# Attention loop of a four-layer MQA/Hedgehog kernel: smaller turns where no other work is mixed in, feature spills issued one transfer per tick, and the state update placed before the query normalization

## The chip, the cores and the metric

The kernel runs on one core of a Trainium2 chip. The metric is the device time of one execution in microseconds. A core has a matrix engine (TensorE, PE in the profile, with its weight loads as PEld), a vector engine (VectorE, DVE), a scalar engine (ScalarE, ACT), GpSimd (POOL) and a sync engine (SyncE, SP) whose queue issues the DMAs of this kernel. Each engine works through its own instructions in order and waits on semaphores that the others set.

## The reference

The input is a sequence of 2048 tokens of width 576. Four residual layers follow each other, A, B, A, B, each on a layer-normalized input. A is attention with 32 query heads of width 18 and one shared key and value head (MQA). B is a linear attention with a learned feature map (Hedgehog).

```python
def _A_ref(x, wq, wk, wv, wo):
    q = (x @ wq).reshape(B, S, H, Dh)          # per head
    k = x @ wk; v = x @ wv                     # one head for all
    scores = einsum("bhqd,bkd->bhqk", q, k) * (Dh ** -0.5)
    p = softmax(scores)
    return einsum("bhqk,bkd->bhqd", p, v) @ wo

def _B_ref(x, wqkv, w_phi, wo):
    q, k, v = x @ wqkv                          # per head
    pq = einsum("bhsd,hdf->bhsf", q, w_phi); pk = einsum("bhsd,hdf->bhsf", k, w_phi)
    phi_q = concat([softmax(pq), softmax(-pq)]); phi_k = concat([softmax(pk), softmax(-pk)])
    kv = einsum("bhsf,bhsd->bhfd", phi_k, v); z = einsum("bhsf->bhf", phi_k)
    return (phi_q @ kv) / (phi_q @ z + 1e-6) @ wo
# x = x + A(ln(x)); x = x + B(ln(x)); x = x + A(ln(x)); x = x + B(ln(x))
```

## The kernel before

The work is done in two passes of one A and one B each. In a pass, `attend` runs the attention of A over 4 chunks of 512 queries and 8 groups of 4 heads in each chunk, 32 groups in all. The first group is done ahead of it, so `attend` has 31 groups. A group goes through 16 tiles of 128 keys. A tile is done in two **units** of two heads: a unit is two score matmuls into one `sc` buffer of PSUM (there are three such buffers), and one exponential on ScalarE from `sc` into a tile `pt` in SBUF (L960, 128x1024). When both units of a tile are done, `values` adds their product with the values to the group's accumulator, four matmuls side by side (L738). 31 groups of 32 units are 992 units in a pass.

The main loop of `attend` (L973 to L982) makes one **step** of six units at a time: three units of scores (`BURST`), the value sums of all tiles that were complete before them, two calls of `tick`, three more units, then `fill`, and value sums again unless `fill` issued a lot of work; then a third `tick`. The order of TensorE's instructions is exactly the order in which this loop records them (`in_order`). The order on the other engines comes from a scheduler. So TensorE's row of work in a step without other work is: three units, two tiles of sums, three units, one tile of sums.

`fill` takes work out of the deque `bulk`: projections and the like that are mixed into the attention. For each finished chunk, `after_chunk` puts `chunk_work` into `bulk`. It makes the output projection of A for the chunk (`output`, 8 fills), turns the residual into the tokens of B (`flip_tokens`, `fetch_tokens`, `split_tokens`), and then runs `mix`: for each of the 4 token tiles the keys, the values and the queries of B (2 fills each), the state update (`update_state`, 32 small matmuls on L526 and an addition to `kv` on VectorE), the softmax of the query features (`feature_end`) and the transfer of the features to DRAM (`block_transpose`: a transposition on VectorE and four DMAs, `phi<-pht` in the profile). All this uses one spare PSUM bank at a time. Weights for it are loaded by generators in the deque `loads`, one step of a generator per tick; a weight tile comes by DMA into one of two buffers `wstage` and is split by VectorE into a high and a low part (`wchi` and `wclo` for the query weights `wpq` and the output weights `wo`).

When a group's sums are done, `finish_group` copies the accumulator to `osb` (L870), gets the reciprocal of the denominators by way of DRAM (`rd`, `den_rows`, `parts`), multiplies, and sends the result with four to nine DMAs into `on` (`pack`, `on<-parts`). It goes on by one stage per tick. After the last group of a chunk it waits some more ticks and then puts the chunk's work into `bulk`. The queries of the next group are fetched when a group's first scores are recorded (`qst<-qd`, `qst<-mxd`, eight DMAs); there are two buffers `qst`.

So there are two kinds of steps: mixed ones, while `bulk` holds work, and pure ones, while it is empty. The fourth chunk of a pass is done after the attention in another way that the change does not touch.

Of the kernel before, what the change touches and what calls it, by code (L numbers as in the profile page):

```python
# [60 lines left out]
def kernel(ctx, tc, x_in, wq, wk, wv, wo, wqkv, w_phi, wob, out):  # L61
# [459 lines left out]
    def update_state(e, vb, st, ps):  # L521
        phi = e.rearrange("p h s d -> p (h s d)")
        pk = ps.tile([P, NG * 2 * DH], F32, name="ps")
        for h in range(H):
            g, j = divmod(h, GH)
            T.matmul(pk[32 * j : 32 * j + 32, g * 2 * DH : (g + 1) * 2 * DH],  # L526
                     vb[:, h * (DH + 1) : h * (DH + 1) + 32], phi[:, h * 2 * DH : (h + 1) * 2 * DH],
                     start=True, stop=True)
            if j == GH - 1 and g < NG - 1:
                yield 145  # L530
        with tc.high_priority():
            V.tensor_add(st["kv"], st["kv"], pk)
        yield -145
# [41 lines left out]
    def block_transpose(blocks, src, dst):  # L575
        V.transpose(blocks, src)
        for q in range(P // 32):
            rows = slice(q * 32, (q + 1) * 32)
            nc.sync.dma_start(dst[:, rows].rearrange("(b f) t -> f b t", f=32),
                              blocks[rows, :].rearrange("f (b t) -> f b t", t=32))  # L580

    def flip_tokens(i):
        rstd, bias = ln_stats([i])[i]
        xn = bw.tile([P, H, 2, DH], F32, name="featq").rearrange("p h s d -> p (h s d)")[:, :D]
        V.tensor_scalar(xn, xres[i], rstd, bias, op0=ALU.mult, op1=ALU.add)
        blocks = bw.tile([P, NKG, P], F32, name="pht").rearrange("p a b -> p (a b)")
        block_transpose(blocks[:, :D], xn, flipped[i % TPC])

    def fetch_tokens(i):
        xt = bw.tile([P, KT * P], F32, name="xn").rearrange("p (a b) -> p a b", b=P)  # L590
        src = flipped[i % TPC]
        nc.sync.dma_start(xt[:, 0:4, :], src[:512].rearrange("(k p) t -> p k t", p=P))
        for half in range(2):
            nc.sync.dma_start(xt[half * 64 : half * 64 + 64, 4, :], src[512:])
        return xt
# [5 lines left out]
        V.tensor_sub(xs[64:P, 4, :], xt[64:P, 4, :], xs[64:P, 4, :].bitcast(F32))  # L601
        return xs

    def mix(tiles, fetched, xs, st, ps, spill, loads):
        for n, i in enumerate(tiles):
            ek, eq = (bw.tile([P, H, 2, DH], F32, name=tag) for tag in ("featk", "featq"))
            vb = yield from keys_values(i, xs, ek, st, ps, V)
            while loads:
                yield STAGE
            yield from queries(xs, eq, st, ps, V)  # L610
            if n < len(tiles) - 1:
                xs = split_tokens(fetched)
                if n < len(tiles) - 2:
                    fetched = fetch_tokens(tiles[n + 2])
            for b in range(2):
                feature_end(eq, b, V)
            yield from update_state(ek, vb, st, ps)
            blocks = bw.tile([P, NKG, P], F32, name="pht").rearrange("p a b -> p (a b)")
            block_transpose(blocks[:, : 2 * D], eq.rearrange("p h s d -> p (h s d)"), spill[i])

    def last_mix(n, i, stats, st, sp, ps, spill):
        xn = layer_norm(i, stats, bw if n % 2 else sp, A, "xn" if n % 2 else "xo")
# [222 lines left out]
    def attend(layer, st, a1o, extra, after_chunk, chunks):  # L845
# [11 lines left out]
        with ctx1:  # L857
# [5 lines left out]
                def tile(self, shape, dtype, name):  # L863
                    return bank(*homes[1], shape)
            acc, on = {groups[0]: st["acc0"]}, {}
            urgent, bulk, loads = deque(), deque(), deque()

            def finish_group(c, g):
                osb = a1.tile([P, CW], F32, name="osb", bufs=1)
                V.tensor_copy(osb, acc[c, g])  # L870
# [12 lines left out]
                parts = a1.tile([P, 2, CW], F32R, name="parts", bufs=1)  # L883
                den = parts[:, 1, :].bitcast(F32)
                nc.sync.dma_start(den, rows[:, None, :].to_broadcast([GH, 32, CW]))
                yield STAGE
                yield STAGE
                V.tensor_mul(osb, osb, den)  # L888
                split(parts[:, 0, :], parts[:, 1, :], osb, V, V)
                yield STAGE  # L890
                yield STAGE
                pack(on[c].bitcast(F32), parts.bitcast(F32), g)
                if g == NG - 2:
                    for _ in range(6):
                        yield STAGE
                    bulk.append(after_chunk(c, on[c], Spare(), loads))
                yield STAGE

            def values(c, g, t, pt):
# [13 lines left out]
                urgent.append(f)  # L913

            def tick():
                for queue in (urgent, loads):
                    if queue and next(queue[0], DONE) is DONE:
                        queue.popleft()

# [51 lines left out]
                    in_order()  # L971

            while at[0] < len(units):  # L973
                sums(scores(BURST))
                tick()
                tick()
                ready = scores(BURST)
                spent = fill()
                in_order()
                if spent < HEAVY:  # L980
                    sums(ready)
                tick()  # L982
# [5 lines left out]
            for queue in (bulk, loads):  # L988
                for gen in queue:
                    run(gen)  # L990

# [71 lines left out]
    for layer in range(LAYERS):  # L1063
# [3 lines left out]
        with tc.tile_pool(name="a1o", bufs=2) as a1o:  # L1067
# [27 lines left out]
            def after_chunk(c, on, ps, loads, layer=layer):  # L1095
                return chunk_work(c, on, ps, loads, layer)

            def chunk_work(c, on, ps, loads, layer):
# [12 lines left out]
                loads.append(load_wpq())  # L1111
                yield from mix(tiles, fetched, xs, st, ps, spills[layer], loads)
                loads.append(load_wo())

            attend(layer, st, a1o, extra, after_chunk, chunks)
# [109 lines left out]
```

## Time and profile before

| | us |
|---|---|
| median of 3 runs | 2777.47 (2773.98 to 2779.59) |
| the profiled execution | 2775.14 |
| its span | 2773.3 |
| busy in it: TensorE / ScalarE / VectorE | 2646.9 / 2190.3 / 1243.3 |
| exponentials of the attention (L960) | 1984, 1874.8 busy |
| mean granted TensorE clock | 0.989 |

In a row of the waits stand the engine and line, whom it waited for, the microseconds in total, how often, and the longest. A row of a group ends in busy time and mean duration in nanoseconds, then the idle time before its instructions with what ended it. In a timeline stand the start, the duration of the merged row, engine, line, operation, tiles and count, and in brackets the idle time before. A row of windows has the stretch, its length, and for each engine its busy time with the number of instructions; behind them the granted clock, the DMA share and GB/s.

### The profile page before, as it was taken

Reading aid. Unit: us, or ns where it says so; the run is one execution under the profiler, and the core shown is the slowest. Engines: PE = TensorE matmul, PEld = TensorE weight load, DVE = VectorE, ACT = ScalarE, POOL = GpSimd, SP = SyncE. Lnnn points to the kernel's source line nnn. Section 1 sums busy time; section 2 is a strip of 40 time slices with the busy share of each in tenths; the row PEclk is TensorE's granted clock in tenths of the full one; section 3 lists DMA queues with packets and bytes.
Section 4 is the critical chain, followed back from the end, with each engine's and each line's share of the span. In section 5 each row is a group of like instructions: output and inputs, shape, how many; then the busy total and the mean of one; then the engine's idle time right before and its main releaser. Section 6 shows DMA issues by size and latency. Waiting matters only on the chain. (4 is left out here: it accounts for less than half of the span.)

```text
span 2773.3 us, 55536 instructions
## 1 busy us (share of the span) xinstructions
PE 2646.9 (95%) x22094; PEld 1459.3 (53%) x22094; DVE 1243.3 (45%) x2899; ACT 2190.3 (79%) x2644; POOL 86.1 (3%) x123
## 2 busy tenths in 40 slices
PE   6989999999999999999999888999999999999999
PEld 5733335453555355568986222355535553555788
DVE  7421224453355335558764300145434543454775
ACT  4679998899899989964345899989998999899421
POOL 1000000000000000004000000000000000000110
PEclk9999999999999999999999999999999999999999
DMA  5322232222232223234632311132123212321444
GB/s 185 108 64 65 69 95 77 76 53 61 67 90 53 61 73 84 53 95 115 184 122 92 89 37 35 37 103 58 40 69 101 61 39 70 102 53 44 111 118 138
DMA packets 355814, 224.97 MB, mean 81 GB/s; under 512 B 206874, under 2 KB 288986, under 8 KB 355546
## 3 DMA queue, kind: packets, MB, share of 16 engines
q1 hardware_dynamic: 355546, 221.31, 28.8%
q8 instruction: 178, 2.92, 0.4%
q14 instruction: 90, 0.74, 0.1%
HBM read 132.88 MB, written 67.03 MB: 72 GB/s over the span
## 5 line engine op out<-in xcount | busy, mean ns | idle before, releaser
L960 ACT ACTIVATE pt<-sc 128x1024 f32<-128x1024 f32 x1984 | 1874.8, 1030 | 175.5 <-PE sc L451 155.7
L451 PE MATMUL sc<-qst,kst 56*128 56x512 f32 x3840 | 694.6, 448 | 54.7 <-ACT pt L960 54.4
L451 PEld LDWEIGHTS sc<-qst,kst 56*128 56x128 f32 x3840 | 319.2, 184 | 609.8 <-ACT pt L960 567.1
L738 PE MATMUL acc<-pt,vst 128*32 128x512 f32 x4096 | 498.4, 604 | 0.5 <-DVE xn L296 0.4
L738 PE MATMUL ps<-pt,vst 128*32 128x512 f32 x3840 | 463.2, 598 | 0.8 <-DVE featk L314 0.8
L738 PEld LDWEIGHTS acc<-pt,vst 128*32 128x32 f32 x4096 | 110.3, 110 | 225.6 <-issue 219.5
L738 PEld LDWEIGHTS ps<-pt,vst 128*32 128x32 f32 x3840 | 101.4, 109 | 202.0 <-issue 197.6
L205 PE MATMUL ps<-wahi,xs 128*128 128x288 f32 x801 | 173.9, 303 | 1.0 <-ACT xs L137 0.9
L205 PEld LDWEIGHTS ps<-wahi,xs 128*128 128x128 f32 x801 | 130.9, 188 | 10.1 <-issue 6.8
L205 PE MATMUL ps<-walo,xs 128*128 128x288 f32 x445 | 130.7, 296 | 0.0
L229 POOL TENSOR_TENSOR rstd<-var,neghalf 128x1 f32<-128x1 f32 (+1 forms) x56 | 33.3, 594 | 2484.6 <-DVE var L227 1703.4
L888 DVE TENSOR_TENSOR osb<-osb,parts 128x512 f32<-128x512 f32 x62 | 42.7, 689 | 142.8 <-DMA parts<-den_rows 142.8
L355 PE MATMUL ps<-xsc,wbhi 128*128 128x256 f32 x513 | 97.2, 285 | 5.2 <-DVE xsc L140 2.3
L205 PE MATMUL ps<-wchi,xs 128*128 128x288 f32 x414 | 91.8, 306 | 2.2 <-DVE wchi L139 1.8
L137 ACT ACTIVATE xs<-ps 128x512 fp32r<-128x512 f32 x34 | 20.3, 596 | 92.9 <-PE ps L248 92.8
L205 PE MATMUL ps<-wchi,on 128*128 128x288 f32 x405 | 89.2, 304 | 0.0
L357 ACT ACTIVATE pcs<-ps 128x256 fp32r<-128x256 f32 x71 | 26.7, 385 | 77.6 <-PE ps L355 72.7
L355 PEld LDWEIGHTS ps<-xsc,wbhi 128*128 128x128 f32 x513 | 82.1, 192 | 6.9 <-DVE xsc L140 2.6
L205 PEld LDWEIGHTS ps<-walo,xs 128*128 128x128 f32 x445 | 83.7, 188 | 0.0
L870 DVE COPY osb<-acc 128x512 f32<-128x512 f32 x32 | 21.9, 684 | 133.4 <-PE acc L738 103.8
L870 DVE COPY osb<-ps 128x512 f32<-128x512 f32 x30 | 20.7, 691 | 133.8 <-PE ps L738 133.8
L355 PE MATMUL ps<-xsc,wblo 128*128 128x256 f32 x285 | 79.0, 284 | 0.0
(320 smaller groups left out, 3480.4 us busy)
## 6 DMA issues: line engine op xcount, KB each, us to landing
qst<-qd SPq DMA_DIRECT2D x360, 72.0 KB
pht<-phi SPq DMA_DIRECT2D x32, 540.0 KB
qd<-pcs SPq DMA_DIRECT2D x64, 256.0 KB
parts<-den_rows SPq DMA_DIRECT2D x62, 256.0 KB
wstage<-folded SPq DMA_DIRECT2D x50, 288.0 KB
on<-parts SPq DMA_DIRECT2D x192, 72.0 KB
phi<-pht SPq DMA_DIRECT2D x96, 144.0 KB
wstage<-in_A_wo_dram SPq DMA_DIRECT2D x32, 288.0 KB
```

The costliest lines, as they stand in the source:

```text
L137: A.activation(dst_hi, src, AF.Copy)
L205: T.matmul(dst, xs[:, slot, :], w[half][:, k, c0 : c0 + HALF], start=(n == 0), stop=(n == last))
L229: G.tensor_tensor(rstd, var, neghalf[:, :n], op=ALU.pow)
L355: T.matmul(po, lhs, xsc[:, slot, :], start=(n == 0), stop=(n == LASTP))
L357: A.activation(pc[:, 0, :], po, AF.Copy)
L451: T.matmul(sc, kst[head_rows(h), t * P : (t + 1) * P], q[head_rows(h), h // 2, :], start=True, stop=True)
L738: T.matmul(acc[32 * j : 32 * j + 32, :], vst[:, t, :], pts[j], start=first, stop=last)
L870: V.tensor_copy(osb, acc[c, g])
L888: V.tensor_mul(osb, osb, den)
L960: A.activation(pt, sc, AF.Exp, scale=SCALE)
```

## The change

Three things are changed.

First, a step of the main loop now looks at `bulk` when it begins. If there is mixed work, it is as before. If there is none, it makes three turns of two units (one tile of scores), one tile of sums and one tick.

Second, `block_transpose` yields after each of its four DMAs. `mix` makes the transposition and the first of them at once and puts the rest into a new deque `slow`, from which each tick takes one. `flip_tokens` still runs all four.

Third, in `mix` the state update is recorded before `feature_end` of the queries instead of behind it.

```diff
@@ block_transpose
             nc.sync.dma_start(dst[:, rows].rearrange("(b f) t -> f b t", f=32),
                               blocks[rows, :].rearrange("f (b t) -> f b t", t=32))
+            yield
@@ mix
+            yield from update_state(ek, vb, st, ps)
             for b in range(2):
                 feature_end(eq, b, V)
-            yield from update_state(ek, vb, st, ps)
             blocks = bw.tile([P, NKG, P], F32, name="pht").rearrange("p a b -> p (a b)")
-            block_transpose(blocks[:, : 2 * D], eq.rearrange("p h s d -> p (h s d)"), spill[i])
+            spilling = block_transpose(blocks[:, : 2 * D], eq.rearrange("p h s d -> p (h s d)"), spill[i])
+            next(spilling)
+            slow.append(spilling)
@@ tick
-                for queue in (urgent, loads):
+                for queue in (urgent, loads, slow):
@@ the main loop of attend
             while at[0] < len(units):
-                sums(scores(BURST))
-                tick()
-                tick()
-                ready = scores(BURST)
-                spent = fill()
-                in_order()
-                if spent < HEAVY:
-                    sums(ready)
-                tick()
+                if bulk:
+                    sums(scores(BURST))
+                    tick()
+                    tick()
+                    ready = scores(BURST)
+                    spent = fill()
+                    in_order()
+                    if spent < HEAVY:
+                        sums(ready)
+                    tick()
+                else:
+                    for n in range(3):
+                        ready = scores(2)
+                        sums(min(ready - 1, done[0] + 2))
+                        tick()
```

On TensorE this is the order in a pure stretch of the second pass, where the first group of `attend` ends (its queries are in `xs`) and the second begins (queries in `qst`). A unit is two rows of L451, a tile of sums is four of L738. Before:

```order
L738 MATMUL acc<-pt,vst 32x512 x4
L451 MATMUL sc<-xs,kst 128x512 x4
L451 MATMUL sc<-qst,kst 128x512 x2
L738 MATMUL acc<-pt,vst 32x512 x8
L451 MATMUL sc<-qst,kst 128x512 x6
L738 MATMUL acc<-pt,vst 32x512 x4
L451 MATMUL sc<-qst,kst 128x512 x6
L738 MATMUL ps<-pt,vst 32x512 x8
```

Now (the line of the sums has moved to L741):

```order
L451 MATMUL sc<-xs,kst 128x512 x4
L741 MATMUL acc<-pt,vst 32x512 x4
L451 MATMUL sc<-qst,kst 128x512 x4
L741 MATMUL acc<-pt,vst 32x512 x4
L451 MATMUL sc<-qst,kst 128x512 x4
L741 MATMUL acc<-pt,vst 32x512 x4
L451 MATMUL sc<-qst,kst 128x512 x4
L741 MATMUL ps<-pt,vst 32x512 x4
```

Blocks of three units and of one or two tiles have become blocks of two units and one tile. The whole order has 204 such turns: 18, 18 and 15 in the three pure stretches of the first pass and 120, 18 and 15 in those of the second.

The mixed work begins elsewhere too, since a step that finds `bulk` empty at its start no longer calls `fill`. The first mixed projection of chunk 0 stands behind 264 units instead of 258, that of chunk 1 behind 522 instead of 516, that of chunk 2 behind 774 as before; the same in both passes. This moves the mixed work against the ends of the groups. On VectorE, this is the place in chunk 0 of the first pass where the last three query weight tiles are split (`wchi`, `wclo`), between the values and the queries of the first token tile; `osb` is the copy of a finished group, `vb` the copy of the two value projections. Before:

```order
L513 COPY vb_2419<-acc 128x16x18 x2
L870 COPY osb<-ps 128x512
L139 CAST wchi<-wstage 128x576
L140 TENSOR_TENSOR wclo_5347<-wstage,wchi 128x576
L139 CAST wchi<-wstage 128x576
L140 TENSOR_TENSOR wclo_5348<-wstage,wchi 128x576
L139 CAST wchi<-wstage 128x576
L140 TENSOR_TENSOR wclo_5348<-wstage,wchi 128x576
L482 COPY featq<-ps 128x16x18
```

Now:

```order
L513 COPY vb_2419<-acc 128x16x18
L873 COPY osb<-ps 128x512
L513 COPY vb_2419<-ps 128x16x18
L139 CAST wchi<-wstage 128x576
L140 TENSOR_TENSOR wclo_5394<-wstage,wchi 128x576
L139 CAST wchi<-wstage 128x576
L140 TENSOR_TENSOR wclo_5395<-wstage,wchi 128x576
L139 CAST wchi<-wstage 128x576
L140 TENSOR_TENSOR wclo_5395<-wstage,wchi 128x576
L881 RECIPROCAL rd<-rd 128x16
L482 COPY featq<-ps 128x16x18
```

The group's copy now stands between the two value copies, no longer between them and the splits. The number of instructions is the same on every engine.

More of the change, by code (lines that the diff above doesn't have):

```diff
@@ L586, in flip_tokens @@
         blocks = bw.tile([P, NKG, P], F32, name="pht").rearrange("p a b -> p (a b)")
-        block_transpose(blocks[:, :D], xn, flipped[i % TPC])
+        run(block_transpose(blocks[:, :D], xn, flipped[i % TPC]))
     def fetch_tokens(i):
@@ L602, in split_tokens, with mix @@
         return xs
-    def mix(tiles, fetched, xs, st, ps, spill, loads):
+    def mix(tiles, fetched, xs, st, ps, spill, loads, slow):
         for n, i in enumerate(tiles):
@@ L865, in attend @@
             acc, on = {groups[0]: st["acc0"]}, {}
-            urgent, bulk, loads = deque(), deque(), deque()
+            urgent, bulk, loads, slow = deque(), deque(), deque(), deque()
             def finish_group(c, g):
@@ L895, in finish_group @@
                         yield STAGE
-                    bulk.append(after_chunk(c, on[c], Spare(), loads))
+                    bulk.append(after_chunk(c, on[c], Spare(), loads, slow))
                 yield STAGE
@@ L987, in attend @@
                 tick()
-            for queue in (bulk, loads):
+            for queue in (bulk, loads, slow):
                 for gen in queue:
@@ L1093, in extra, with after_chunk, chunk_work @@
                 loads.append(load("wv", "b", wqkv, slice(2 * D, 3 * D)))
-            def after_chunk(c, on, ps, loads, layer=layer):
-                return chunk_work(c, on, ps, loads, layer)
-            def chunk_work(c, on, ps, loads, layer):
+            def after_chunk(c, on, ps, loads, slow, layer=layer):
+                return chunk_work(c, on, ps, loads, slow, layer)
+            def chunk_work(c, on, ps, loads, slow, layer):
                 drain(loads)
@@ L1111, in chunk_work @@
                 loads.append(load_wpq())
-                yield from mix(tiles, fetched, xs, st, ps, spills[layer], loads)
+                yield from mix(tiles, fetched, xs, st, ps, spills[layer], loads, slow)
                 loads.append(load_wo())
```

## The prediction

> **What bounds the kernel now.** I read the page first, then the waits of the whole span.
>
> ```profile
> span 2773.3 us, 55536 instructions
> L960 ACT ACTIVATE pt<-sc 128x1024 f32<-128x1024 f32 x1984 | 1874.8, 1030 | 175.5 <-PE sc L451 155.7
> PEld sc L451 <- ACT pt L960: 598.1, 994, 1.7
> ACT pt L960 <- PE sc L451: 155.7, 312, 5.4
> ```
>
> The 1984 exponentials fill 1874.8 of 2773.3 us, so at least two thirds of the span are the two attention loops. There TensorE and ScalarE wait for each other: 598.1 us in the one direction, 155.7 us in the other. Which wait counts depends on the kind of step, so next I read windows: one stretch of mixed steps, one of exactly 14 pure steps (from one step's first exponential to that of the step 14 later).
>
> ```profile
> 1790.00:1856.00 66.00, 66.00 (x498) 35.09 (x494) 29.78 (x68) 58.17 (x62) 2.54 (x4) 1.00 0.35 94
> 1664.11:1745.24 81.13, 72.44 (x504) 22.64 (x504) 7.58 (x14) 78.46 (x85) 0.00 (x0) 1.00 0.12 33
> ```
>
> The first number behind the length is TensorE, the fourth ScalarE. Mixed steps are full on TensorE (66.00 of 66.00): only work or waits of TensorE count there. Pure steps take 81.13 / 14 = 5.795 us, TensorE has 8.7 us to spare, ScalarE is busy for 78.46. The timeline of ScalarE in this stretch, and behind it one from the folding in the first pass:
>
> ```profile
> 1713.54 5.61 ACT L960 ACTIVATE pt<-sc 128x1024 f32<-128x1024 f32 x6 [0.20 <-PE sc L451]
> 1719.33 5.60 ACT L960 ACTIVATE pt<-sc 128x1024 f32<-128x1024 f32 x6 [0.18 <-PE sc L451]
> 221.49 8.38 ACT L960 ACTIVATE pt<-sc 128x1024 f32<-128x1024 f32 x9 [0.26 <-PE sc L451]
> ```
>
> In a pure step ScalarE stops once, for 0.2 us, for a score. Where scores are always ready, nine exponentials take 8.38 us: with 1.03 for one alone, the pitch is (8.38 - 1.03) / 8 = 0.92 us. Six at that pitch are 5.52 us. Why it stops is in the chain of waits:
>
> ```profile
> 1710.64 0.51 PE sc L451 x2
> 1711.15 1.85 PE ps L738 x16
> 1713.00 0.92 PE sc L451 x6
> 1713.96 0.50 issue
> ```
>
> A block of two tiles of sums (1.85 us) stands between two scores. ScalarE's three buffered units are used up 2.76 us after the last buffer came free; the next score begins 0.51 + 1.85 = 2.36 us behind that point and needs about 0.6 us to reach ScalarE (1713.00 to the exponential at 1713.54): 0.2 us late.
>
> **First edit, the turns.** A turn is two units of scores and one tile of sums. On TensorE: the first score follows the sums at once, 0.92 / 3 = 0.31 us; the second waits for a buffer, 0.51 us with its start; the sums take 1.85 / 2 = 0.93 us. That is 1.75 us against two exponentials of 1.84 us, so ScalarE is the slower one. Is a score ever late? Let a buffer come free at 0. The second score of a turn begins there, sums follow until 1.44, the next turn's first score begins at 1.44 and reaches ScalarE at about 2.0. ScalarE wants it after three units, at 2.76. The margin of 0.7 us is larger than the lateness of 0.2 us before, so the stop goes, and with it the restart. I take 5.795 - 5.52 = 0.275 us a step. The order has 204 turns, 68 steps: 68 x 0.275 = **18.7 us**. Bounds: nothing, if the pitch is that of mixed steps (below), and 68 x 0.28 = 19 if every wait goes. What is late next is ScalarE itself; a step can't be shorter than 5.52. Ticks stay at three a step, and all that they advance (reciprocals, loads, query fetches) has whole groups of 29 us and more to land; I cost that at nothing.
>
> **First edit, the shift.** In chunks 0 and 1 the mixed work begins one step later against the ends of the groups. Mixed steps stay as many as before, so this moves only collisions. There are two large ones in the trace. The windows are of the query projections of chunk 0 in both passes, and of chunk 2 in the first pass, over the same two steps:
>
> ```profile
> 494.14:510.86 16.72, 15.39 (x104) 7.42 (x102) 8.71 (x17) 11.99 (x13) 0.00 (x0) 0.90 0.25 74
> 1859.57:1876.20 16.63, 15.39 (x104) 7.42 (x102) 8.71 (x17) 11.99 (x14) 0.00 (x0) 0.90 0.25 73
> 1053.81:1067.13 13.32, 13.32 (x104) 7.09 (x102) 7.98 (x16) 12.00 (x14) 0.00 (x0) 1.00 0.30 92
> ```
>
> Chunk 0 takes 3.40 and 3.31 us more. The timeline of VectorE says why; chunk 0 first, then chunk 2:
>
> ```profile
> 495.67 0.69 DVE L870 COPY osb<-ps 128x512 f32<-128x512 f32 x1 [1.57 <-PE ps L738]
> 496.27 0.45 DVE L139 CAST wchi<-wstage 128x576 fp32r<-128x576 f32 x1
> 500.43 0.46 DVE L139 CAST wchi<-wstage 128x576 fp32r<-128x576 f32 x1 [1.75 <-DMA wstage<-folded]
> 1049.55 0.69 DVE L870 COPY osb<-ps 128x512 f32<-128x512 f32 x1 [2.42 <-PE ps L738]
> 1053.69 0.45 DVE L139 CAST wchi<-wstage 128x576 fp32r<-128x576 f32 x1
> 1057.86 0.46 DVE L139 CAST wchi<-wstage 128x576 fp32r<-128x576 f32 x1 [1.77 <-DMA wstage<-folded]
> ```
>
> In chunk 0 the three splits stand behind the copy of a group that ends in the very step in which TensorE already wants the query weights; the last of them also waits for a transfer that can only start when the first has freed its buffer. In chunk 2 the group ends a step earlier and the same splits are just in time. In the new order chunk 0 has the instructions of chunk 2's order there (copy of values, of the group, of values, then the splits). So I take the whole difference: 3.40 + 3.31 = **6.7 us**; bounds: nothing, and the 6.7.
>
> The second collision is the first output projection of chunk 1, both passes, with chunk 2 of the same pass below each, and SyncE's queue before it:
>
> ```profile
> 695.69:709.98 14.29, 12.83 (x94) 7.05 (x94) 2.32 (x6) 11.44 (x13) 0.00 (x0) 1.00 0.20 55
> 974.52:987.19 12.67, 12.49 (x94) 6.85 (x94) 2.22 (x6) 11.46 (x14) 0.00 (x0) 1.00 0.17 46
> 2060.88:2075.37 14.49, 12.80 (x94) 7.06 (x94) 2.32 (x6) 11.45 (x13) 0.00 (x0) 1.00 0.21 55
> 2339.90:2352.56 12.66, 12.48 (x94) 6.84 (x94) 2.21 (x6) 11.45 (x13) 0.00 (x0) 1.00 0.17 46
> 681.96 0.69 DVE L140 TENSOR_TENSOR parts<-osb,parts 128x512 fp32r<-128x512 f32 x1
> 695.48 1.03 SPq L440 DMA_DIRECT2D qst<-qd  x3
> 696.61 3.40 SPq L819 DMA_DIRECT2D on<-parts  x4
> PE acc L205 <- DMA on<-parts: 1.3, 1, 1.3
> ```
>
> The group's parts are ready at 682.65, but their four transfers stand in SyncE's queue behind query fetches that wait for a buffer until 695.48, so they land at about 702 and the projection waits. The new order still has them behind two such fetches, but the projection comes a step (5.5 us) later, which is more than the wait. I take 1.62 + 1.83 = **3.4 us**; bounds: nothing and 3.4.
>
> **Second and third edit.** Of a feature spill the same four DMAs are issued, a row of 2.5 us for four:
>
> ```profile
> 562.17 1.38 DVE L576 STREAM_TRANSPOSE pht<-featq 128x1152 f32<-128x1152 f32 x1
> 563.48 0.42 DVE L532 TENSOR_TENSOR kv<-kv,acc 128x288 f32<-128x288 f32 x1
> 566.39 0.40 PE L205 MATMUL acc<-wahi,xs 128*128 128x288 f32 x1
> 567.02 2.49 SPq L579 DMA_DIRECT2D phi<-pht  x4
> ```
>
> Their buffer is wanted again seven steps later, which hides the spread. A spill may now stand before a fetch or a weight load, for at most 0.6 us of issue each; those have a step and more in hand. I cost it at nothing, between a loss of 1 us and a gain of 1. The state update is recorded earlier, but the new order of VectorE still has the addition to `kv` behind the transposition in nearly every tile, and TensorE's order is the same. Even now the addition ends at 563.90 and the bank is wanted at 566.39, so moving it earlier frees nobody: nothing again, and if that cover of 2.5 us were gone, 0.4 us a tile over 24 tiles, 10 us at most.
>
> **The sum.** 18.7 + 6.7 + 3.4 = 28.8 us off the profiled 2775.1, which is 2746.3. The median of the runs lies 2.3 us above the profiled one: 2777.5 - 28.8, about **2749 us**. A measurement of this kernel can tell about 0.2%, 5.5 us, from no change.
>
> **Rivals.** *Only the turns pay* (0.17): the scheduler orders VectorE and SyncE anew, and the 10.1 us of collisions come back at other places, say in chunk 1, whose splits also move against the groups. For it: chunk 0 has its stall in both passes by its position alone. Against: chunk 0 takes over an order that ran without one, and in chunk 1 three of the five splits now stand well ahead. Time 2777.5 - 18.7 = 2759.
>
> *ScalarE can't keep the pitch* (0.08). In mixed steps six exponentials take longer:
>
> ```profile
> 1803.20 5.80 ACT L960 ACTIVATE pt<-sc 128x1024 f32<-128x1024 f32 x6 [0.84 <-PE sc L451]
> ```
>
> That is (5.80 - 1.03) / 5 = 0.954 us each. If turns give this pitch, a step is 5.72 us, the gain 68 x 0.075 = 5 us, and with the collisions 15: 2762. Against: those six are paced by scores that arrive late, and nine in a row ran at 0.92. The Trainium skill, "ScalarE: Activation LUTs", section "What ACT_TABLE_LOAD costs", has 186 ns and 0.833 ns an element, less 93 ns back to back: an estimate of 946 ns for 1024 elements, close to this rival. By that rule the turns would bring about 8 us and the total be about 2759; the row of nine at 0.92 disagrees with it.
>
> *The turns slow TensorE's clock* (0.03), the case that ends slower. TensorE now stops in every turn instead of a few times a step. The granted clock is 0.90 in the stalled windows above, and the chain shows what that does to 24 sums:
>
> ```profile
> 1868.47 4.24 PE acc L738 x24
> 1876.66 2.71 PE acc L738 x24
> ```
>
> At 4.24 / 2.71 a turn's sums take 1.45 us, the turn 2.27, the step 6.8: 68 x 1.0 = 68 us lost, 58 net, 2836. It decides once a turn is over 1.93 us, the present 5.795 / 3. Against: the present pure steps have stops of up to 0.4 us at a clock of 1.00, and a turn's stops are of that kind. The Trainium skill, "TensorE: Matmul & The Clock Gate", section "A second HAM failure mode: psum-queue depth-cycling", says that frequent short idles between groups of matmuls can make the clock swing between half and full; the row of 1.00 doesn't show it in this loop.
>
> *The change does nothing* (0.04): turns still meet a wait of 0.2 us a step and the collisions return: 2777.
>
> **How the numbers follow.** The forecast has 0.68. Faster by over 0.2% are the forecast and the first two rivals: 0.93. Within 0.2% is 0.04, slower 0.03. The range reaches down to where other small waits of the attention go too, some 6 us beyond the terms, less 1 us for the spread of the runs, so 2742, and up to 2763, which takes in the first two rivals.
>
> **What would show it.** In pure stretches ScalarE should have no stop before an exponential and 14 steps should take 77 us; TensorE's granted clock should stay 1.00. The windows of chunk 0's queries should be near 13.3 us, chunk 1's first output near 12.7. Wrong would be stops of ScalarE for scores in pure steps, a pitch of 0.95, or a new wait of TensorE for `wchi` or `on` in chunk 1.

## The result: the turns pay more than forecast, and new stalls take all of it

The changed kernel takes 2780.93 us (median of 14 runs, 2775.63 to 2785.91), the kernel before 2778.26 (14 runs) beside it. The ratio is 1.0013, 95% interval 1.0005 to 1.0022: slower by about 3.6 us (the medians themselves lie 2.7 apart). The forecast was 2749, range 2742 to 2763. The profiled execution of the changed kernel took 2777.95 us.

Its page first, with the group of the attention's exponentials (now L963):

```profile
span 2776.2 us, 55537 instructions
L963 ACT ACTIVATE pt<-sc 128x1024 f32<-128x1024 f32 x1984 | 1867.9, 1115 | 171.6 <-PE sc L451 152.4
```

ScalarE's idle time before the exponentials hardly fell, from 175.5 to 171.6 us. The windows of the changed kernel show what went well: 14 pure steps, the query projections of chunk 0 in both passes, the first output projection of chunk 1 in the first pass. Since the mixed work begins a step later, the last three rows start one step of the attention later than the prediction's windows and hold the same work.

```profile
1664.22:1741.22 77.00, 77.00 (x506) 22.27 (x504) 7.80 (x15) 77.00 (x86) 0.00 (x0) 1.00 0.12 35
497.74:511.07 13.33, 13.33 (x104) 7.12 (x102) 7.65 (x15) 11.99 (x13) 0.00 (x0) 1.00 0.44 122
1859.68:1874.28 14.60, 13.76 (x104) 7.21 (x102) 7.64 (x15) 12.00 (x14) 0.00 (x0) 1.00 0.36 105
707.69:720.84 13.15, 12.73 (x96) 6.86 (x94) 1.55 (x5) 11.93 (x14) 0.00 (x0) 1.00 0.17 49
```

ScalarE is busy for 77.00 of 77.00 us at a TensorE clock of 1.00: 5.50 us a step, from 5.795. Chunk 0's query projections fell from 16.72 to 13.33 us in the first pass and from 16.63 to 14.60 in the second; chunk 1's first output from 14.29 to 13.15.

To find where that went, I cut each pass of the loop into steps of six exponentials (step k holds number 6k to 6k+5 of the pass, up to the next one's start) and took the differences, after minus before:

| us | pass 1 | pass 2 |
|---|---|---|
| pure steps, and all that no other row names | -6.4 | -16.4 |
| steps 54 and 55 (before: chunk 0's query projections) | -3.4 | -1.9 |
| steps 85 and 86 (before: chunk 1's first output) | -2.4 | -2.6 |
| chunk 0, steps 56 to 62 | +3.6 | +2.1 |
| steps 63 to 68 | +5.4 | +5.4 |
| steps 69 to 79 | +5.9 | +4.9 |
| chunk 1, steps 87 to 122 | +3.7 | +6.6 |
| all of the loop | +6.4 | -1.9 |

The gains add up to 33.1 us, the losses to 37.6. Of the losses 35.2 sit at steps 57, 64, 78 and 121 and the step behind each. Not all of that is a stall: the mixed work of chunks 0 and 1 stands a step later, so steps 78 and 121 are mixed steps where pure ones were, and that alone is 0.9 us each (6.70 us without a stall, in e13_mulbehind below, against 5.79). So about 34 us are stalls. In these steps the last work of a token tile, its query features and state update, falls together with the end of a group or with the stages that finish it. There are two kinds. The first is at step 64; TensorE, then VectorE, of the first pass:

```profile
564.38 0.77 PE L526 MATMUL acc<-featk,vb 128*32 128x36 f32 x64
568.07 1.94 PE L741 MATMUL acc<-pt,vst 128*32 128x512 f32 x8 [2.92 <-DVE kv L532]
569.94 1.65 PE L451 MATMUL sc<-qst,kst 56*128 56x512 f32 x6
565.51 0.76 DVE L496 TENSOR_TENSOR featq<-featq,fz 128x576 f32<-128x576 f32 x1
566.30 1.38 DVE L576 STREAM_TRANSPOSE pht<-featq 128x1152 f32<-128x1152 f32 x1
567.61 0.42 DVE L532 TENSOR_TENSOR kv<-kv,acc 128x288 f32<-128x288 f32 x1
```

The state update sits in the spare bank. With each new group the two banks change roles, so a group's first sums need the bank that was spare. Here a group begins right behind the state update, and TensorE waits 2.92 us until VectorE has done the normalization, the transposition and only then the addition that frees the bank. Behind the wait the eight rows of sums (one tile, whose four matmuls show as eight rows in a trace) take 1.94 us and the six scores 1.65, where 1.06 and 0.96 are usual.

The second kind, at steps 57, 78 and 121, goes over three engines; here step 57: SyncE's queue, VectorE, ScalarE, TensorE.

```profile
506.35 0.58 SPq L888 DMA_DIRECT2D parts<-den_rows  x1
511.44 0.69 DVE L891 TENSOR_TENSOR osb<-osb,parts 128x512 f32<-128x512 f32 x1 [2.55 <-DMA parts<-den_rows]
513.24 0.45 DVE L482 COPY featq<-ps 128x288 f32<-128x288 f32 x1
515.76 0.45 DVE L487 TENSOR_TENSOR featq<-featq,fmax 128x288 f32<-128x288 f32 x1
516.25 0.68 ACT L489 ACTIVATE featq<-featq 128x576 f32<-128x576 f32 x1 [2.31 <-DVE featq L487]
517.89 0.50 PE L451 MATMUL sc<-qst,kst 56*128 56x512 f32 x2 [1.19 <-ACT pt L963]
```

The multiplication of a finished group by its reciprocal denominators (L891) stands on VectorE ahead of the query features, and it waits for a transfer that lands 4.5 us after its issue has ended. The features come late, ScalarE stops in front of their exponential (2.31 us) with the attention's exponentials behind it, and TensorE runs out of free `sc` buffers. The waits of ScalarE for these features over the whole span, before and after:

```profile
ACT featq L489 <- DVE featq L487: 15.1, 13, 2.6
```

```profile
ACT featq L489 <- DVE featq L487: 30.6, 17, 3.5
```

### The profile page after: what moved, and what is told of

Same layout as the page of the kernel before. It is cut to its first block, busy times and chain, and to the rows that moved or that the text cites. A ratio compares the mean times of both kernels' runs of the same rounds, so it can differ in the third digit from the quotient of the medians.

```text
span 2776.2 us, 55537 instructions
## 1 busy us (share of the span) xinstructions
PE 2679.4 (97%) x22094; PEld 1460.2 (53%) x22094; DVE 1241.8 (45%) x2899; ACT 2181.8 (79%) x2644; POOL 85.9 (3%) x123
## 3 DMA queue, kind: packets, MB, share of 16 engines
q8 instruction: 178, 2.92, 0.4%
## 5 line engine op out<-in xcount | busy, mean ns | idle before, releaser
L963 ACT ACTIVATE pt<-sc 128x1024 f32<-128x1024 f32 x1984 | 1867.9, 1115 | 171.6 <-PE sc L451 152.4
L451 PE MATMUL sc<-qst,kst 56*128 56x512 f32 x3840 | 716.6, 457 | 25.3 <-ACT pt L963 24.2
L451 PEld LDWEIGHTS sc<-qst,kst 56*128 56x128 f32 x3840 | 326.1, 185 | 634.4 <-ACT pt L963 580.7
L741 PE MATMUL acc<-pt,vst 128*32 128x512 f32 x4096 | 510.2, 612 | 6.2 <-DVE kv L532 5.8
L741 PE MATMUL ps<-pt,vst 128*32 128x512 f32 x3840 | 471.8, 599 | 0.8 <-DVE featk L314 0.8
L741 PEld LDWEIGHTS acc<-pt,vst 128*32 128x32 f32 x4096 | 108.9, 111 | 225.0 <-issue 213.0
L741 PEld LDWEIGHTS ps<-pt,vst 128*32 128x32 f32 x3840 | 97.0, 109 | 186.3 <-issue 180.6
L891 DVE TENSOR_TENSOR osb<-osb,parts 128x512 f32<-128x512 f32 x62 | 42.8, 690 | 136.6 <-DMA parts<-den_rows 136.6
L137 ACT ACTIVATE xs<-ps 128x512 fp32r<-128x512 f32 x34 | 20.3, 596 | 92.6 <-PE ps L248 92.4
L205 PE MATMUL ps<-wchi,xs 128*128 128x288 f32 x378 | 83.6, 306 | 0.8 <-DVE wchi L139 0.4
L262 DVE TENSOR_TENSOR xc<-xc,ps 128x288 f32<-128x288 f32 x61 | 27.2, 447 | 118.3 <-PE ps L205 118.3
```

What stands on the lines that cost most here:

```text
L137: A.activation(dst_hi, src, AF.Copy)
L205: T.matmul(dst, xs[:, slot, :], w[half][:, k, c0 : c0 + HALF], start=(n == 0), stop=(n == last))
L262: V.tensor_add(xr, xr, po)
L451: T.matmul(sc, kst[head_rows(h), t * P : (t + 1) * P], q[head_rows(h), h // 2, :], start=True, stop=True)
L741: T.matmul(acc[32 * j : 32 * j + 32, :], vst[:, t, :], pts[j], start=first, stop=last)
L963: A.activation(pt, sc, AF.Exp, scale=SCALE)
```

## Experiments

All ratios are to the kernel before, run on the same chip (medians 2776.7 to 2778.4), with 95% intervals.

| run | us | ratio |
|---|---|---|
| e1_turns | 2808.88 | 1.0111 (1.0096 to 1.0127) |
| e2_noshift | 2788.48 | 1.0037 (1.0023 to 1.0051) |
| e3_shift | 2828.47 | 1.0179 (1.0162 to 1.0196) |
| e4_rest | 2792.79 | 1.0055 (1.0041 to 1.0069) |
| e5_kvfirst | 2776.77 | 0.9993 (0.9984 to 1.0001) |
| e6_noshift_fetch | 2756.74 | 0.9915 (0.9902 to 0.9928) |
| e7_pool | 2783.05 | 1.0015 (1.0002 to 1.0028) |
| e8_all | 2751.23 | 0.9905 (0.9891 to 0.9919) |
| e9_fetch | 2755.74 | 0.9919 (0.9904 to 0.9934) |
| e10_before_fetch | 2783.03 | 1.0018 (1.0009 to 1.0027) |
| e11_noshift_all | 2762.08 | 0.9943 (0.9930 to 0.9957) |
| e12_turns_clean | 2754.60 | 0.9922 (0.9908 to 0.9936) |
| e13_mulbehind | 2766.37 | 0.9965 (0.9952 to 0.9979) |
| e14_kvfetch | 2747.61 | 0.9893 (0.9878 to 0.9908) |
| e15_turns_fetch | 2753.60 | 0.9912 (0.9897 to 0.9927) |

### Which part makes the stalls

**e1_turns**: the changed kernel without its second and third edit.

> This is the changed kernel with only its first edit: the turns of pure steps, with the later start of the mixed work that comes with them. The state update is again recorded behind the query normalization and a spill issues its four DMAs at once. Theory A (the mixed work, which begins one step later in chunks 0 and 1, now meets the ends of the groups at its state updates, and that eats what the turns bring): 2778 to 2784 us, the same as the changed kernel within 3 us. The new stalls, about 8.5 to 10.5 us in steps 57, 64, 78 and 121 of both passes, are still there. Rival B (the spread spills or the earlier state update make those stalls): they are gone, and the time is 2778.3 less 23 us of turns less 10 us of old collisions, about 2746.

Neither: 28 us slower than the changed kernel. The stalls of theory A are there, and others with them, the largest at the first output projection of chunk 2 (steps 128 and 129: 13.6 + 8.1 us, from 6.0 + 6.6 before). The waits of TensorE, and SyncE's queue:

```profile
PE acc L205 <- DMA on<-parts: 12.3, 2, 6.3
```

```profile
986.70 0.66 SPq L440 DMA_DIRECT2D qst<-qd  x2
987.45 0.59 SPq L887 DMA_DIRECT2D parts<-den_rows  x1
994.25 3.42 SPq L821 DMA_DIRECT2D on<-parts  x4
```

The fetch of the next queries waits in the queue for its buffer until 986.70, and the group's denominators wait behind it. In the changed kernel they pass ahead of that fetch, at 962.66:

```profile
962.66 0.59 SPq L888 DMA_DIRECT2D parts<-den_rows  x1
```

**e3_shift**: the kernel before with only the mixed work of chunks 0 and 1 a step later.

```diff
-                    for _ in range(6):
+                    for _ in range(9 if c < 2 else 6):
```

> This is the kernel before with one number changed: the last group of chunks 0 and 1 waits three ticks more, one step, before its chunk's work goes into the deque of mixed work, so it begins at 264 and 522 units as in the changed kernel. No turns, no spread spills, no earlier state update. Theory A (the later start alone makes the new stalls): slower. The new stalls of the changed kernel add up to about 36 us above their neighbours over both passes, the old collisions of 10 us go: 2778 + 36 - 10 = about 2804 us, 2795 to 2812. Rival B: the old collisions go and nothing comes in their place, 2768 us. Rival C (the stalls need the shift and the turns or the state update together): between, 2772 to 2790.

Theory A in sign, and twice the size: 52 us slower. Steps 57, 64, 78 and 121 take 8.2, 10.4, 9.6 and 9.5 us in the first pass, and the stall of chunk 2's output is there as in e1_turns. The later start alone makes the stalls; neither turns nor spills are needed.

**e4_rest**: the kernel before with the second and third edit.

> This is the kernel before with the second and third edit alone: spills issue one DMA per tick and the state update is recorded ahead of the query normalization; the main loop is as before. Theory A: 2778 us within 2, nothing happens, as these two were costed at nothing. Rival B (one of the two makes the new stalls): 2795 to 2812 us.

Slower by 16 us, though the mixed work begins where it did. The third edit has no part in it: this program and the changed kernel, each built with and without it, have the same order of instructions on all five engines. So it is the spread spills. They bring the second kind of stall to steps 77 and 120, the last token tiles of chunks 0 and 1 (9.4 + 8.1 and 9.8 + 8.0 us, from 6.8 + 5.8 and 6.7 + 5.8). VectorE and ScalarE at step 77, and behind them the same two instructions of VectorE in the kernel before, where the multiplication waits almost as long but behind the features:

```profile
653.89 0.69 DVE L891 TENSOR_TENSOR osb<-osb,parts 128x512 f32<-128x512 f32 x1 [2.63 <-DMA parts<-den_rows]
654.50 0.45 DVE L487 TENSOR_TENSOR featq<-featq,fmax 128x288 f32<-128x288 f32 x1
654.99 0.68 ACT L489 ACTIVATE featq<-featq 128x576 f32<-128x576 f32 x1 [3.20 <-DVE featq L487]
```

```profile
651.34 0.45 DVE L487 TENSOR_TENSOR featq<-featq,fmax 128x288 f32<-128x288 f32 x1
655.70 0.69 DVE L888 TENSOR_TENSOR osb<-osb,parts 128x512 f32<-128x512 f32 x1 [2.35 <-DMA parts<-den_rows]
```

**e2_noshift**: the changed kernel, with the mixed work at its old place.

```diff
                         ready = scores(2)
-                        sums(min(ready - 1, done[0] + 2))
+                        spent = fill() if n == 2 else 0
+                        in_order()
+                        if spent < HEAVY:
+                            sums(min(ready - 1, done[0] + 2))
```

> This is the changed kernel, but a pure step calls fill in its third turn, so that the mixed work begins at 258, 516 and 774 units as in the kernel before; the turns, the spread spills and the earlier state update stay. Theory A (the later start makes the new stalls): the four new stalls of each pass go, the old collisions come back (chunk 0's query weights 6.7 us, chunk 1's first output 3.4 us), and what is left is the gain of the turns, which measured 5.79 to 5.42 us a step in the first pass and 5.79 to 5.50 in most of the second: about 2778.3 - 23 = 2755 us, between 2750 and 2760. Rival B (spills or state update make the stalls): about the time of the changed kernel, 2775 to 2783.

Neither in full. Steps 57 and 64 are short again (6.0 us each), which is theory A. But the stalls of e4_rest are there, and the old wait of chunk 1's first output has grown: steps 85 and 86 take 15.9 + 8.7 us in place of 7.7 + 6.6. The turns bring TensorE to the projection sooner, while the parts hang behind a query fetch as in e1_turns; SyncE's queue, then TensorE:

```profile
696.03 0.30 SPq L440 DMA_DIRECT2D qst<-qd  x1
696.42 0.59 SPq L888 DMA_DIRECT2D parts<-den_rows  x1
703.88 3.35 SPq L822 DMA_DIRECT2D on<-parts  x4
709.31 0.58 PE L205 MATMUL acc<-wchi,on 128*128 128x288 f32 x1 [8.27 <-DMA on<-parts]
```

So the edits don't add up. The turns with their shift cost 32 us, the spread spills 16, and both together 3 to 4, because the spread spills let transfers pass the blocked fetch just where the shift had put them behind it.

### The stalls one by one

**e5_kvfirst**: the addition to `kv` first (`st["added"]` is its name).

```diff
+            feature_end(eq, 0, V)
+            n0 = len(traced(nc))
+            feature_end(eq, 1, V)
+            tc.add_manual_dep(traced(nc)[n0 + 1], st["added"], NOSYNC, reason="order")
```

> This is the changed kernel with the addition to kv set ahead of the second half of the query normalization and of the transposition on VectorE. Theory: at step 64 of both passes the first sums of the next group wait for the bank that this addition frees; TensorE then lost 5.4 us per pass with the slower clock behind it (10.43 + 7.42 us for two steps that take 6.4 + 6.0 + 6.6 less one elsewhere). With the addition ahead the bank is free about when the state update ends: step 64 about 6.5 us, both passes together 10.8 us, so 2781 - 11 = 2770 us. The stalls at steps 57, 78 and 121 have another cause and stay. Rival (the clock or the group's end itself makes step 64 long): no change, 2778 to 2784.

Step 64 does what the theory says, from 10.43 + 7.42 to 6.89 + 6.00 us, but the time gains only 4 us on the changed kernel, not the 11 expected. Other work comes late instead. At steps 55 and 56 of the first pass (8.4 + 8.2 us) it is the query weights: the last cast to `wchi` waits 3.90 us for its transfer, and TensorE for the cast. At step 121 of the second (11.7 us) it is the features, for which ScalarE waits 5.5 us. Why the transfer came later here is not shown.

**e7_pool**: `tensor_mul(osb, osb, den)` and the split behind it on GpSimd.

> This is the changed kernel with the multiplication of a finished group by its reciprocal denominators, and the split behind it, on GpSimd instead of VectorE. Theory: at steps 57, 78 and 121 VectorE stood up to 2.6 us at this multiplication for a transfer (parts<-den_rows), and the query features behind it came late to ScalarE, which stopped in front of their exponential, and TensorE with it; off VectorE, these stops go. They cost about 3.6 + 5.5 + 2.2 us in the first pass and 2.1 + 4.4 + 4.9 in the second, 22.7 us: 2781 - 23 = 2758 us, with the stall at step 64 left. Rival (the features are late because VectorE has too much work there, not because it waits): a part goes, 2765 to 2778. GpSimd's own time for these three operations is not in any row; if it is over some 8 us, the output projections wait for it and the time is over 2781.

No gain. ScalarE's wait for the features falls from 30.6 to 20.3 us, but the query weights come late instead, as the waits of TensorE show; step 55 takes 11.8 us. GpSimd's three operations take 3.3 us (1.29, 0.67 and 1.32).

```profile
PE ps L205 <- DVE wchi L139: 10.7, 6, 3.9
```

**e13_mulbehind** tells the causes of the second kind apart: the multiplication is recorded five ticks later and set behind the features on VectorE (`st["feat"]` is the last L487 recorded by then). The ticks behind it become fewer in turn, so that the mixed work stays in place.

```diff
                 V.tensor_mul(osb, osb, den)
+                if "feat" in st:
+                    tc.add_manual_dep(traced(nc)[-1], st["feat"], NOSYNC, reason="order")
```

> This is the changed kernel with the multiplication of a finished group by its reciprocal denominators recorded five ticks later and set behind the last query features recorded by then on VectorE; the query fetch stays early and the mixed work stays where the change put it. In VectorE's order it now stands behind the second half of the query features at steps 57, 78 and 121, where it stood ahead of them. Theory A (VectorE's order is the cause: it waits there for parts<-den_rows with the features queued behind): these stalls go, 2781 - 23 = 2758 us, step 64 stays at 10.4. Theory B (the early fetch in SyncE's queue is the cause, and the late fetch of e9_fetch cured it by freeing that queue): no gain, 2775 to 2783.

Theory A for the stalls. Steps 57, 78 and 121 fall to 6.42, 6.70 and 6.70 us in both passes, with the query fetch as early as before, while step 64 stays at 10.3 and 9.3. On VectorE the multiplication no longer has to wait (lines are three or four further down in this kernel), and ScalarE's wait is below that of the kernel before:

```profile
514.95 0.45 DVE L489 TENSOR_TENSOR featq<-featq,fmax 128x288 f32<-128x288 f32 x1
515.75 0.69 DVE L895 TENSOR_TENSOR osb<-osb,parts 128x512 f32<-128x512 f32 x1
```

```profile
ACT featq L492 <- DVE featq L489: 13.8, 11, 2.4
```

The attention loops got 22.9 us shorter, the 23 expected. The median fell by 14.6 only, 8 us short of theory A's number: in the profiles 10.8 us came back outside the loops, 3.4 between them and 6.1 behind the second. What costs them there stays open.

### The query fetch

**e6_noshift_fetch**: e2_noshift with the fetch later.

```diff
-                    if t == 0 and hh == 0 and n < len(groups) - 1:
+                    if t == 4 and hh == 0 and n < len(groups) - 1:
```

> This is the kernel of the run e2_noshift, with the queries of the next group fetched when the scores of a group's fifth tile are recorded instead of its first. Theory: at step 85 the first output projection of chunk 1 waited 8.3 us for parts of the last group, whose transfer (parts<-den_rows) stood in SyncE's queue behind a query fetch that waited for its buffer until 696.03; with later fetches nothing stands ahead of it, so steps 85 and 86 fall from 15.9 + 8.7 to about 6.0 + 6.6 in both passes: 24 us, 2788 - 24 = 2764 us. The stalls at steps 77 and 120 stay. Rival (the group's end comes too close to the projection in any order): under 8 us gained, 2780 to 2788.

32 us faster than e2_noshift, 8 more than expected: step 85 takes 6.5 us, and steps 77 and 120 lost part of their stalls too.

**e9_fetch**: the changed kernel with that line alone.

> This is the changed kernel with the later query fetch alone (at a group's fifth tile). It tells which of the three measures of the run e8_all matters. Theory A (the fetch that blocks SyncE's queue also delays the transfers rd, den_rows and parts of a finished group, and so makes VectorE stand at steps 57, 78 and 121): these stalls go, step 64 stays, 2781 - 23 = 2758 us. Theory B (the fetch has no part in these stalls, only VectorE's order has): 2774 to 2782 us.

Theory A's number, 25 us faster than the changed kernel. But e13_mulbehind shows that the blocked queue is not the cause by itself. The later fetch has changed VectorE's order: at step 57 the multiplication now stands behind the features, the transposition and the state, and waits there without harm, while step 64 keeps its stall.

```profile
516.92 1.38 DVE L576 STREAM_TRANSPOSE pht<-featq 128x1152 f32<-128x1152 f32 x1
518.22 0.41 DVE L532 TENSOR_TENSOR kv<-kv,ps 128x288 f32<-128x288 f32 x1
520.81 0.69 DVE L891 TENSOR_TENSOR osb<-osb,parts 128x512 f32<-128x512 f32 x1 [2.18 <-DMA parts<-den_rows]
```

**e10_before_fetch**: the kernel before with that line.

> This is the kernel before with the later query fetch alone. It shows how much of the gain of the runs with this edit has nothing to do with the turns. Theory: it takes away the wait of chunk 1's first output projection, 1.62 + 1.83 us, and of the chunk 0 query weights about 1 us a pass as in the run e6_noshift_fetch (9.17 + 6.54 in place of 8.53 + 8.19): 2778 - 5.5 = 2772 us. Rival: the fetch moves other transfers into the way: over 2778.

The rival: slower by 5 us. TensorE's wait for chunk 1's parts is gone (step 85 6.2 us), but steps 72 and 77 take 8.4 and 8.3. The late fetch is not a gain of its own.

**e12_turns_clean**: the turns, the old place of the mixed work, the late fetch, nothing else.

> This is the changed kernel without its second and third edit, with fill in the third turn of a pure step (the mixed work begins where it did before) and the later query fetch: of the change only the turns are left. Against the run e10_before_fetch, which has the same places of the mixed work and the same fetch, it measures the turns alone. Theory: 23 us, worked out from the steps, so about 2772 - 23 = 2749 us. Rival (the turns cost something that the steps do not show): less than 15 us between the two.

2754.6 against the 2783.0 of e10_before_fetch: 28 us for the turns, 24 of them in the two loops of the profiles.

**e15_turns_fetch**: e1_turns with the late fetch.

> This is the kernel of the run e1_turns, in effect the changed kernel without the spread spills, with the later query fetch. It tells whether the spread spills have a worth of their own or only let transfers pass the blocked query fetch. Theory A (only the latter): with the fetch out of the way the spills matter little, 2756 us within 4, as e9_fetch. Theory B (the spills have a worth of their own at steps 55 to 57 and 63, where e1_turns lost some 10 us a pass): 2770 to 2785.

Theory A: 2753.6, 55 us less than e1_turns and 2 less than e9_fetch with the spread spills, which is no clear difference. (The third edit, which moves nothing, is still in it.) Their worth was in passing the blocked fetch.

**e8_all**, **e11_noshift_all** and **e14_kvfetch** put measures together: all three on the changed kernel, all three at the old place, and the two that proved themselves.

> This is the changed kernel with all three: the addition to kv ahead, the multiplication by the denominators on GpSimd, the later query fetch. Theory: the stalls at steps 57, 64, 78 and 121 all go and the order of SyncE's queue does no harm: 2781 - 11 - 23 = 2747 us. Rival (another order brings other collisions, as each of these kernels did): over 2765.

> This is the kernel of the run e6_noshift_fetch with the addition to kv ahead and the multiplication by the denominators on GpSimd as in the run e8_all. Theory: the rest of the stalls at steps 77 and 120 (8.2 and 7.2 to 7.4 us) goes, about 4.5 us: 2757 - 4.5 = 2752 us, and chunk 0's query weights stay late. Rival (GpSimd brings collisions of its own as in e7_pool): 2757 or more.

> This is the kernel of the run e9_fetch (later query fetch) with the addition to kv ahead of the second half of the query normalization. e9_fetch kept the stall at step 64 in both passes (10.2 + 6.3 and 10.4 + 7.4). Theory: these become 6.9 + 6.0 as in e5_kvfirst and e8_all, 3.6 + 4.9 us less, and step 121 stays: 2756 - 8.5 = 2747 us. Rival (the new order of VectorE brings late features or weights elsewhere, as in e5_kvfirst): 2756 or more.

e8_all came 4 us above its number, e11_noshift_all 10 above, within its rival's range; that GpSimd is to blame there was not tested apart. e14_kvfetch is the fastest of all, 1.07% below the kernel before, and within 1 us of what the causes add up to. Its span, then TensorE and VectorE at step 64, then the window of steps 64 and 65:

```profile
span 2747.2 us, 55492 instructions
```

```profile
564.35 1.06 PE L744 MATMUL acc<-pt,vst 128*32 128x512 f32 x8 [0.55 <-DVE kv L532]
563.84 0.45 DVE L532 TENSOR_TENSOR kv<-kv,acc 128x288 f32<-128x288 f32 x1
565.38 1.38 DVE L577 STREAM_TRANSPOSE pht<-featq 128x1152 f32<-128x1152 f32 x1
```

```profile
559.05:571.95 12.90, 12.32 (x154) 5.87 (x152) 7.54 (x17) 11.89 (x14) 0.00 (x0) 1.00 0.32 84
```

The wait for the bank fell from 2.92 to 0.55 us, and the sums behind it run at their usual 1.06.

## Why the prediction was wrong, step by step

- **The turns**, 18.7 us: right in kind, too small. 68 steps at 0.275 are 18.7 us; the table has 22.8, and the loops of e12_turns_clean got 24 shorter than those of e10_before_fetch. The pitch of 0.92 us, from nine exponentials in a row, is 0.903 in pure steps of the first pass (5.42 us for six) and 0.917 in most of the second; why they differ I don't know. The rivals of a pitch of 0.95 and of a slower clock in the turns are out (77.00 us for 14 steps at 1.00).
- **The two collisions that go**, 10.1 us: right in kind, a little too large. Over the same work 7.9 us went: 5.4 of the 6.7 at chunk 0's queries, 2.5 of the 3.4 at chunk 1's output. In the second pass step 55 keeps 8.0 us, as the last cast to `wchi` there waits 3.51 us for its transfer. At chunk 1 nothing is left of the wait; but the first mixed step behind the turns is longer, for chunk 2's output, which did not move, takes 13.08 us now and took 12.67.
- **"Mixed steps stay as many as before, so this moves only collisions. There are two large ones in the trace."** This is the step that failed. I priced the collisions that the trace of before has, and none that the new place would make. In the changed kernel these are about 34 us of stalls, and e3_shift shows that the later place alone makes them: without the other edits it costs 52 us. The rival *Only the turns pay* had the kind right (collisions come back elsewhere) and capped it at 10 us.
- **"Moving it earlier frees nobody"** and its cover of 2.5 us: I asked when the next projection wants the bank, at 566.39. Where a group begins there, its first sums want it at once. With the slower sums and scores behind the wait this cost 5.4 us in each pass.
- **The second edit**, between a loss of 1 us and a gain of 1: wrong by more than ten times. I counted 0.6 us of issue and left out what the order of SyncE's queue decides. It loses 16 us at the old place (e4_rest) and gains 28 at the new one (changed kernel against e1_turns).
- **The third edit**, nothing: right, it moves no instruction.

## What to carry to other kernels

When a change moves work against a periodic event, go through the new order at every place where the two now meet, and ask on each engine what the first instruction waits for and what stands behind it; the trace of before only shows the collisions that go. An instruction that waits for a transfer costs little by itself and much through what is queued behind it; here it helped to put it behind the work that was ready, and to issue a fetch only when its buffer is about to come free. Edits that touch a queue's order are to be measured both apart and together, since their effects don't add.

## What the runs showed of the hardware

TensorE's clock suffers from shorter stops than I had thought, but not from each of them. Three windows of the changed kernel follow: steps 57 and 58 and steps 64 and 65 of the first pass, with a granted clock of 0.89 and 0.81, and steps 57 and 58 of the second pass, with 1.00. Behind them are the first two tiles of sums after the stops at step 57, from the timeline, first pass, then second, and the longest stop of the second.

```profile
511.07:527.12 16.05, 14.03 (x154) 6.00 (x152) 9.04 (x19) 11.88 (x13) 0.00 (x0) 0.89 0.33 81
560.41:578.26 17.85, 14.93 (x154) 6.31 (x152) 7.46 (x17) 11.99 (x14) 0.00 (x0) 0.81 0.37 81
1874.28:1888.94 14.66, 12.54 (x154) 5.82 (x152) 9.04 (x19) 11.88 (x14) 0.00 (x0) 1.00 0.36 85
```

```profile
520.44 3.19 PE L741 MATMUL acc<-pt,vst 128*32 128x512 f32 x16
1883.53 1.92 PE L741 MATMUL acc<-pt,vst 128*32 128x512 f32 x16
1881.27 0.50 PE L451 MATMUL sc<-qst,kst 56*128 56x512 f32 x2 [1.29 <-ACT pt L963]
```

At step 57 of the first pass TensorE stops for 1.19 us and twice for 0.41, 2.0 us within 3.0, and the two tiles of sums then take 3.19 us. In the second pass it stops for 1.29 us and twice for 0.41, and the same sums take 1.92. So the length of the stops does not decide by itself. The half-speed periods of this trace start whole multiples of 3.41 us apart (519.63, 567.41 and 666.40 in the first pass). Cut into stretches of that length, the stops of the first pass lie in one stretch, which a slow one follows, and those of the second are divided over two:

```profile
516.21:519.63 3.42, 1.50 (x12) 0.37 (x4) 2.86 (x6) 3.38 (x5) 0.00 (x0) 1.00 0.51 137
519.63:523.04 3.41, 3.32 (x18) 0.88 (x18) 1.02 (x2) 2.78 (x4) 0.00 (x0) 0.50 0.56 96
1878.13:1881.55 3.42, 2.13 (x76) 1.00 (x74) 2.89 (x8) 1.92 (x3) 0.00 (x0) 1.00 0.43 99
1881.55:1884.96 3.41, 2.58 (x22) 0.79 (x20) 2.44 (x3) 3.41 (x5) 0.00 (x0) 1.00 0.40 104
```

TensorE is idle for 1.92 us of the stretch ahead of the slow one, and for 1.29 and 0.84 where none follows. In the loops of all 17 traces, cut in this way, a slow stretch never follows one with less than 34% idle, and some with up to 56% idle have none behind them; no run varies this by itself, so the limit stays open. So what a stall costs depends also on where its stops fall in these stretches: step 58 takes 7.58 us in the first pass and 6.01 in the second. The single stop of 0.55 us in e14_kvfetch left the clock at 1.00. The Trainium skill, "TensorE: Matmul & The Clock Gate", section "Why this matters for your kernels", advises against idle gaps of over some 3 us. Here stops with a longest of 1.19 us were enough in one place, so a limit on the single gap does not describe this trace.
